# Attention, MoE and FFN on one core: x^T from quarter-array products with a PSUM bank per batch, late arrivals at fixed places, and the third pair's steps later

## The chip, the cores and the metric

The kernel runs on one core of a Trainium2 chip, in one launch. The metric is the device time of that launch in microseconds (us), the median of several executions; lower is better. Engines are named as in the profile: PE is TensorE's matmul side and PEld its weight loads, DVE is VectorE, ACT is ScalarE, POOL is GpSimd, and SP is SyncE, which here issues nearly all DMAs in one queue.

## The reference, cut to what matters

Three layers follow each other: linear attention over 4 batches of 8 heads, 576 tokens and 64 dimensions; a dense mixture of 8 experts with Sinkhorn routing; and a feed-forward network. Tokens are 2304 = 4 x 576, the model width is 512 = 8 x 64.

```
q_s = exp(q - max(q, -1)); q_s /= sum(q_s, -1) + 1e-9        # over the 64 dims
k_s = exp(k - max(k, 2));  k_s /= sum(k_s, 2) + 1e-9         # over the 576 tokens
kv  = einsum('bhsd,bhse->bhde', k_s, v)                      # 64 x 64 for each batch and head
x   = einsum('bhsd,bhde->bhse', q_s, kv) -> (2304, 512)
P   = exp(x @ w_gate - max); 8 times: P /= rows, P /= columns, P *= N / E
out = sum over e of P[:, e] * (relu(x @ w1[e]) @ w2[e])      # w1[e] 512 x 1024, w2[e] 1024 x 512
h   = out @ w_in                                             # 512 x 2048
y   = (h * clip(h + 3, 0, 6) / 6) @ w_out                    # 2048 x 512
```

## The kernel before, in words

The batches are taken two at a time: `attention(0)` (`t0`) holds batches 0 and 1, `attention(1)` (`t1`) batches 2 and 3. The two batches of a pair lie in the two halves of the 128 partitions when kv and x are made. The 18 token tiles form 6 groups of 3 tiles (384 columns), and the groups form three pairs, `PAIRS = [(0, 1), (3, 4), (2, 5)]`. Groups 0 to 2 belong to `t0`, groups 3 to 5 to `t1`, so that the third pair (p = 2) needs both. A column chunk `c` (0 to 3) is 128 of x's 512 columns, that is two heads.

x^T of one `(c, g)` is made by `xset`: q of a group is normalised on POOL (`qn`), transposed on PE (`qtr`, three 128x128 transposes into one PSUM bank), copied by ACT, and multiplied by the scaled kv. Before, that kv lies in `bds`, a block-diagonal array with zeros off its diagonal blocks: four f32 matmuls of 128 rows by 64 columns with 192 moving columns fill one PSUM bank.

Every product of the MoE uses a seven-product (Strassen-like) scheme on halves, with operands split into a high and a low f16 part. `forms(p, ...)` makes the seven x operands of a pair from the x^T banks (`plain` makes a fresh bank, `onto` adds another operand to it by an identity matmul on PE, `out_` writes the high part by ACT and the low part by DVE). The third pair's are combined by `combine_steps` from copies. `w1_steps` and `w2_steps` do the same for a slice of weights: a load into `raw` or `acc`, a maximum over it (`am_a`, `am_b`), a maximum across partitions by a PE broadcast (`across_max`: the column goes to PE as `cm_...`, and DVE reduces the bank), a power of two as the scale (`pow2`), and splits, high by ACT and low by DVE (L217).

The work is a list of steps `(s, p)`: slice `s` of 16 MoE slices and then 4 FFN slices, pair `p`. A step is two up bursts of seven products each (`up_burst`, banks X, Y, Z, or A to D in the FFN), and the down tiles (`y`) of the step ahead of it. All other work hangs on the products: after each one `tick()` takes `rate` entries of the list `ticks`, and one of `side` or `back`. `rate` is 3 in (0, 0), 2 in (1, 0) and then 1. A `None` in a list is a tick in which nothing is issued. In the first six steps of the order the Tile scheduler places instructions; from there on (`tc.manual_schedule()`) they stand as written.

Ahead of (0, 0) stands a prologue: k's maxima and transposes, `ksub`, `kexp`, q's softmax (`qmax`, `qsub`, `qexp`, `qsum`), kv on PE, the first weights' scale, `kvout`, `kvmax` and `kvkeep`, and then `forms` of the first pair. `t1`'s own chain (k, q, kv) runs beside (0, 0) and (1, 0), then `second_pair` makes the second pair's x operands; it ends when (0, 1) starts. PSUM: `ps_u` holds the banks A to D, `ps_d` two banks for `y`, and `ps_m` two banks for everything else (`kT`, `kv`, `qT`, x, forms of the second pair, `cm_...`, Sinkhorn's `csp`).

Of the kernel before, what the change touches and what calls it, by code (L numbers as in the profile page):

```python
# [43 lines left out]
def tile_attention_moe_ffn(  # L44
# [81 lines left out]
    bds = cpool.tile([P, 2, NKC, P], F32, name="bds")  # L126
# [135 lines left out]

    def w1_steps(s, first=False):
# [16 lines left out]
        if first:  # L280
            scale = w_scale(f"a{s}_", st, s, TOP1)
            scale[-1] = (lambda f=scale[-1]: (f(), res[s].__setitem__("s1", st["s"])))
            return load, scale, [
                tt(S1, A[1, 0], A[1, 1], "tensor_add"), tt(S2, S1, A[0, 0], "tensor_sub"),
                tt(A[1, 0], A[0, 0], A[1, 0], "tensor_sub"),
            ], [
                sp(QA11, A[0, 0]), sp(QS2, S2), sp(QS1, S1), sp(QA12, A[0, 1]),
                lambda: (tt(A[0, 1], A[0, 1], S2, "tensor_sub")(), sp(QA22, A[1, 1])()),
                sp(QS3, A[1, 0]), sp(QS4, A[0, 1]),
            ]  # L290
        steps = [load, None, None, None] + w_scale(f"a{s}_", st, s, TOP1)
# [10 lines left out]
    def w2_steps(s, flat=raw):  # L302
# [10 lines left out]
        steps = [load, None, None, None] + w_scale(f"b{s}_", st, s, TOP2, flat)  # L313
# [91 lines left out]
    qbuf = view(half(acc[:, NJ // 2 :, :]), 0, [P, H, QR, D])  # L405

    kt = view(xbuf, X_W, [P, H, QR, D])
# [3 lines left out]
    def attention(pr):  # L411
# [3 lines left out]
        first = pr == 0  # L415
        def rows(src, i):
# [12 lines left out]

        def load_q():  # L430
            load(qbuf, q, slice(0, NKC))
# [21 lines left out]
        def kmax(c):  # L453

            kh = kt[:, 2 * c : 2 * c + 2]
            l1 = view(scr, (c % 2) * DM, [P, 2, 4, D])
# [4 lines left out]
                wide[4][:, c * P : (c + 1) * P].rearrange("p (h d) -> p h d", d=D), l1[:, :, 0], kh[:, :, 8]  # L461
# [14 lines left out]
        def kback(cs):  # L476
# [5 lines left out]
            for n, c in enumerate(cs):  # L482
# [5 lines left out]
                t["kb", c] = ps[:, n * P : (n + 1) * P]  # L488

        def ksub(c):  # L490
            hs = slice(2 * c, 2 * c + 2)
            nc.vector.tensor_tensor(
                out=kt[:, hs], in0=kt[:, hs],
                in1=t["kb", c].rearrange("p (h d) -> p h d", d=D).unsqueeze(2).to_broadcast([P, 2, QR, D]),
# [24 lines left out]
        def kvout():  # L519
# [5 lines left out]
            for j in range(2):  # L525
                for i in range(2):
                    a = slice(i * D, (i + 1) * D)
                    nc.vector.tensor_tensor(
                        out=bds[a, i, :, j * D : (j + 1) * D], in0=t["kv"][j][a, :, :D],
                        in1=rz[a, j].unsqueeze(2).to_broadcast([D, NKC, D]), op=ALU.mult,  # L530
                    )

        def kvmax():
            t["am"] = col("kvm")
            nc.vector.tensor_reduce(
                out=t["am"], in_=bds.rearrange("p i c m -> p (i c m)"), axis=AX, op=ALU.max, apply_absolute_value=True
            )

        def kvkeep():
            nc.vector.tensor_copy(mx[:, pr : pr + 1], st["mm"])  # L540
            pow2(st["mm"], sx[:, pr, :], TOP1)
            nc.scalar.activation(bds[:, 0], bds[:, 0], AF.Copy, scale=sx[:, pr, 0:1])
            nc.vector.tensor_scalar_mul(bds[:, 1], bds[:, 1], sx[:, pr, 0:1])
# [8 lines left out]
        grows = lambda g: slice(gl(g) * GJ, (gl(g) + 1) * GJ)  # L552

        def qmax(g):
            if "qm" not in t:
                t["qm"] = sm.tile([P, H, QR], F32, tag="qm", name=f"qm{pr}", bufs=2)
            nc.vector.tensor_reduce(
                out=t["qm"][:, :, grows(g)], in_=qbuf[:, :, grows(g), :], axis=AX, op=ALU.max
            )

        def qsub(g, eng=nc.vector):
            qh = qbuf[:, :, grows(g), :]
# [3 lines left out]
        def qexp(g):  # L566
            qh = qbuf[:, :, grows(g), :].rearrange("p h r d -> p h (r d)")
            nc.scalar.activation(qh, qh, AF.Exp)

        def qsum(g):  # L570
            if "qs" not in t:
                t["qs"] = sm.tile([P, H, QR], F32, tag="qm", name=f"qs{pr}", bufs=2)
                t["qr"] = sm.tile([P, H, QR], F32, tag="qr", name=f"qr{pr}", bufs=1)
            sv, rv = t["qs"][:, :, grows(g)], t["qr"][:, :, grows(g)]
            nc.vector.tensor_reduce(out=sv, in_=qbuf[:, :, grows(g), :], axis=AX, op=ALU.add)
            nc.vector.tensor_scalar_add(sv, sv, 1e-9)
            nc.vector.reciprocal(rv, sv)
# [743 lines left out]
```

## Time and profile before

| | before |
|---|---|
| device time, median of 3 executions | 1901.04 us (1900.40 to 1901.06) |
| profiled execution, device time | 1901.46 us |
| its span in the profile | 1899.7 us |
| busy: PE / DVE / ACT / POOL | 1845.8 / 1178.0 / 865.8 / 611.1 us |
| mean granted clock of TensorE | 0.991 |

The device time is 1.8 us longer than the span. Busy times are sums over the whole span: they don't tell what ends a wait in one stage. The tables by stretch show the share of each engine in a stretch, the timelines show single instructions with what ended the idle time ahead of them, and the tables of waits sum such idle time by the instruction that waited and by the one that released it. A granted clock (PEclk) of 1.00 is the upper of TensorE's two levels, 2.4 GHz, and 0.50 the lower, 1.2 GHz.

### The profile page before, as it was taken

Reading aid. Unit: us, or ns where it says so; the run is one execution under the profiler, and the core shown is the slowest. Engines: PE = TensorE matmul, PEld = TensorE weight load, DVE = VectorE, ACT = ScalarE, POOL = GpSimd, SP = SyncE. Lnnn points to the kernel's source line nnn. Section 1 sums busy time; section 2 is a strip of 40 time slices with the busy share of each in tenths; the row PEclk is TensorE's granted clock in tenths of the full one; section 3 lists DMA queues with packets and bytes.
Section 4 is the critical chain, followed back from the end, with each engine's and each line's share of the span. In section 5 each row is a group of like instructions: output and inputs, shape, how many; then the busy total and the mean of one; then the engine's idle time right before and its main releaser. Section 6 shows DMA issues by size and latency. Waiting matters only on the chain.

```text
span 1899.7 us, 26823 instructions
## 1 busy us (share of the span) xinstructions
PE 1845.8 (97%) x10596; PEld 976.5 (51%) x10596; DVE 1178.0 (62%) x2109; ACT 865.8 (46%) x1653; POOL 611.1 (32%) x582
## 2 busy tenths in 40 slices
PE   4999999999999999999999999999999999999999
PEld 2555554555555555555555555555555555555554
DVE  8875736565655556565656565565635796768554
ACT  3754434444444444443434444444434466535432
POOL 4342234233342333333333423242332333313121
PEclk8999999999999999999999999999999999999999
DMA  9200001111111202112011111121100100000001
GB/s 294 95 24 1 1 23 56 40 40 56 40 56 40 78 25 71 43 35 73 23 56 39 56 40 58 37 78 33 46 28 1 45 23 23 23 23 23 1 28 72
DMA packets 48430, 87.72 MB, mean 46 GB/s; under 512 B 12208, under 2 KB 12208, under 8 KB 48304
## 3 DMA queue, kind: packets, MB, share of 16 engines
q1 hardware_dynamic: 48304, 86.01, 13.6%
q8 instruction: 83, 1.36, 0.3%
q14 instruction: 43, 0.35, 0.1%
HBM read 72.89 MB, written 13.11 MB: 45 GB/s over the span
## 4 chain that ended last, share of the span: by engine, by line
PE 84%; DVE 11%; ACT 2%; issue 1%; DMA 1%; POOL 0%; SPq 0%; DVEq 0%; ACTq 0%; POOLq 0%
PE y L1028 44%; PE X L928 18%; PE Y L928 9%; PE Z L928 5%; DVE w1buf L217 2%; PE B L928 2%; PE C L928 2%; PE A L928 2%; DVE r L936 1%; PE D L928 1%; DVE acc L1038 1%; DVE g L953 1%; DVE scr L391 1%; DVE xbuf L387 1%; DVE w2buf L217 1%
## 5 line engine op out<-in xcount | busy, mean ns | idle before, releaser
L1028 PE MATMUL y<-w2buf,h 128*128 128x512 f16 x4320 | 992.1, 379 | 0.1
L928 PEld LDWEIGHTS <-w1buf 128*128 128x128 f16 x5040 | 491.1, 98 | 366.4 <-issue 16.4
L1028 PEld LDWEIGHTS <-h 128*128 128x128 f16 x4320 | 422.1, 98 | 470.7 <-issue 4.5
L960 POOL TENSOR_TENSOR h<-r,h 128x384 f16<-128x384 f32 x288 | 273.9, 952 | 869.6 <-ACT h L959 787.5
L928 PE MATMUL X<-xbuf,w1buf 128*128 128x384 f16 x2304 | 440.3, 327 | 1.6 <-ACT r L941 1.1
L941 ACT ACTIVATE r<-X 128x384 f32<-128x384 f32 x384 | 187.0, 487 | 509.7 <-PE X L928 500.2
L1038 DVE SCALAR_TENSOR_TENSOR acc<-y,cf,acc 128x512 f32<-128x512 f32 x252 | 188.0, 746 | 214.3 <-PE y L1028 214.3
L928 PE MATMUL Y<-xbuf,w1buf 128*128 128x384 f16 x1152 | 220.1, 327 | 1.6 <-DVE r L936 0.8
L936 DVE SCALAR_TENSOR_TENSOR r<-Y,r 128x384 f32<-128x384 f32 x192 | 106.0, 552 | 75.5 <-PE Y L928 40.0
L958 ACT ACTIVATE r<-r 128x384 f32<-128x384 f32 x192 | 99.9, 520 | 113.3 <-DVE r L936 112.5
L959 ACT CAST h<-r 128x384 f16<-128x384 f32 x288 | 146.9, 510 | 7.9
L955 POOL TENSOR_TENSOR h<-g,h 128x384 f16<-128x384 f32 x72 | 67.5, 937 | 255.6 <-ACT h L954 200.4
L928 PE MATMUL Z<-xbuf,w1buf 128*128 128x384 f16 x576 | 110.9, 327 | 0.0
L936 DVE SCALAR_TENSOR_TENSOR r<-Z,r 128x384 f32<-128x384 f32 x96 | 53.0, 552 | 91.4 <-PE Z L928 89.4
L962 ACT ACTIVATE h<-r 128x384 f16<-128x384 f32 x96 | 50.2, 522 | 93.1 <-DVE r L936 93.0
L954 ACT CAST h<-g 128x384 f16<-128x384 f32 x96 | 48.9, 511 | 90.6 <-DVE g L953 90.5
L963 DVE SCALAR_TENSOR_TENSOR h<-r,h 128x384 f16<-128x384 f32 x96 | 56.6, 590 | 51.8 <-ACT h L962 51.8
L952 ACT ACTIVATE g<-r,three,zi 128x384 f32<-128x384 f32 x96 | 67.5, 704 | 6.7 <-DVE r L936 5.8
L953 DVE SCALAR_TENSOR_TENSOR g<-g,r 128x384 f32<-128x384 f32 x96 | 60.4, 631 | 13.8 <-ACT g L952 11.1
L936 DVE SCALAR_TENSOR_TENSOR r<-B,r 128x384 f32<-128x384 f32 x48 | 26.6, 554 | 63.6 <-PE B L928 62.0
L928 PE MATMUL C<-xbuf,w1buf 128*128 128x384 f16 x288 | 54.8, 327 | 3.6 <-DVE r L936 3.6
L928 PE MATMUL B<-xbuf,w1buf 128*128 128x384 f16 x288 | 54.6, 326 | 1.7 <-DVE r L936 1.6
(631 smaller groups left out, 1610.7 us busy)
## 6 DMA issues: line engine op xcount, KB each, us to landing
raw<-in_moe_w_dram SPq DMA_DIRECT2D x31, 1024.0 KB, 5.9
scr<-in_moe_w_in_dram SPq DMA_DIRECT2D x16, 512.0 KB, 4.3
scr<-in_moe_w_out_dram SPq DMA_DIRECT2D x16, 512.0 KB, 3.7
acc<-in_q_dram SPq DMA_DIRECT2D x4, 1152.0 KB, 8.4
out_dram<-acc SPq DMA_DIRECT2D x18, 256.0 KB, 2.0
win<-scr SPq DMA_DIRECT2D x16, 256.0 KB, 3.3
wout<-scr SPq DMA_DIRECT2D x16, 256.0 KB, 2.1
raw<-win SPq DMA_DIRECT2D x4, 1024.0 KB, 5.0
```

Source lines behind the costliest of these rows:

```text
L217: nc.vector.scalar_tensor_tensor(out=lo, in0=src, scalar=scale, in1=hi, op0=ALU.mult, op1=ALU.subtract)
L928: nc.tensor.matmul(bank[b], w[:, i, wi, c, fs], x[:, i, xi, c, :], start=(first and n == 0), stop=(last and n == 5), skip_group_check=True,)
L936: nc.vector.scalar_tensor_tensor(out=o, in0=bank[b], scalar=sign * H_DOWN, in1=i1, op0=ALU.mult, op1=ALU.add)
L941: nc.scalar.activation(o, bank[b], fn, scale=H_DOWN)
L952: nc.scalar.activation(r, c, AF.Relu, scale=zi, bias=three)
L953: nc.vector.scalar_tensor_tensor(out=r, in0=r, scalar=6.0 * KAPPA, in1=c, op0=ALU.min, op1=ALU.mult)
L955: eng.tensor_sub(h[:, 1, :], r, h[:, 0, :])
L958: nc.scalar.activation(c, c, AF.Relu)
L959: nc.scalar.copy(h[:, 0, :], c)
L960: eng.tensor_sub(h[:, 1, :], c, h[:, 0, :])
L1028: nc.tensor.matmul(ps, hs[grp][fc][:, hi, ts_], w[:, wi, fc, :], start=(n == 0), stop=(n == 11))
L1038: nc.vector.scalar_tensor_tensor(out=acc[:, j, :], in0=ps, scalar=cf, in1=acc[:, j, :], op0=ALU.mult, op1=ALU.add)
```

## The change

Three edits go together.

1. `bds` is gone. `kvs` holds the scaled kv of both batches without zeros (half the elements, and `kvout`, `kvmax`, `kvkeep` work on half). `xset` now takes two chunks and two banks: each matmul uses 64 rows by 64 columns, the row half is the batch, and each batch has its own bank. `forms` works on a pair of banks with 128x6x64 views of the operands. The number of PE matmuls is the same.
2. The third pair's part of `t0` (group 2: its softmax, its normalising, its products) moves out of the prologue and of (0, 0) into `third_pair`, where `t1`'s group 5 is made. The four `scaled` passes of ACT are dropped, since x is scaled as it leaves PSUM. The last third of q's rows is loaded by itself into `qlast`. `late()` has ACT write one column of head 0's place in it before the DMAs of that head.
3. Loads and maxima get other places. `t1`'s k and v loads stand behind the load of the second slice's w1. Slice 0's w2 has its room in another part of `acc`, and its steps stand after the forms in the prologue. `kmax` takes several chunks at a time. `fill` gives five empty ticks instead of three behind the loads of slices 2 and 3. The step order is (0,0), (1,0), (0,1), (1,1), (0,2), (1,2).

```diff
@@ w1_steps, w2_steps
+    def fill(s):
+        return [None] * (5 if s in (2, 3) else 3)
-        steps = [load, None, None, None] + w_scale(f"a{s}_", st, s, TOP1)
+        steps = [load] + fill(s) + w_scale(f"a{s}_", st, s, TOP1)
@@ attention(pr)
             for j in range(2):
-                for i in range(2):
-                    a = slice(i * D, (i + 1) * D)
-                    nc.vector.tensor_tensor(
-                        out=bds[a, i, :, j * D : (j + 1) * D], in0=t["kv"][j][a, :, :D],
-                        in1=rz[a, j].unsqueeze(2).to_broadcast([D, NKC, D]), op=ALU.mult,
-                    )
+                nc.vector.tensor_tensor(
+                    out=kvs[:, :, j * D : (j + 1) * D], in0=t["kv"][j][:, :, :D],
+                    in1=rz[:, j].unsqueeze(2).to_broadcast([P, NKC, D]), op=ALU.mult,
+                )
...
-        def xset(ps, c, g):
-            p3 = ps.rearrange("p (r n) -> p r n", n=P)
-            q3 = t["qT", c, g].rearrange("p (r n) -> p r n", n=P)
+        def xset(b, cs, g):
+            for n, c in enumerate(cs):
+                q3 = t["qT", c, g].rearrange("p (r n) -> p r n", n=P)
+                for i in range(2):
+                    ai = slice(i * D, (i + 1) * D)
+                    o = b[i].rearrange("p (c r n) -> p c r n", c=2, n=QP)
+                    for j in range(2):
+                        aj = slice(j * QP, (j + 1) * QP)
+                        nc.tensor.matmul(
+                            o[aj, n], kvs[ai, c, aj], q3[ai, :, aj], start=(n == 0), stop=(n == 1),
+                            skip_group_check=True,
+                        )
...
             return [
-                plain(cp, ga, QB11), f_t1, plain(cp + 2, gb, QB22), f_on(QT2, [(minus, QT1)]),
-                plain(cp + 2, ga, QB21), f_on(QT4, [(minus, QB21)]), f_on(QT3, [(plus, QB21), (minus, QB11)]),
+                plain(low, ga, QB11), plain(low, gb, QT1, [(minus, QB11)]), plain(high, ga, QB21),
+                plain(high, gb, QB22), f_on(QT2, [(minus, QT1)]), f_on(QT3, [(minus, QB11)]),
+                f_on(QT4, [(plus, QB11), (minus, QB21)]),
             ]
@@ beside(t1)
+        every = tuple(range(NKC))
+        steps += [
+            lambda: (t["kmax"](every), t["ktr"](every)), K("qmax", ga), lambda: (t["mT"](every, t["kT"]), t["kback"](every)),
+            K("qsub", ga), lambda: (t["ksub"]((0, 1)), t["kexp"](0), t["kexp"](1)), K("qexp", ga),
+            lambda: (t["ksub"]((2, 3)), t["kexp"](2), t["kexp"](3)), K("qmax", gb), K("qsub", gb), K("qexp", gb),
+        ]
@@ third_pair
-    def third_pair(t):
+    def third_pair(t0, t1):
...
-        steps = group_steps(t, gb)
+        steps = [rooms(t0)] + group_steps(t0, ga)
+        steps += t0["items"]([((cp, cp + 2), ga, two(2 * cp), rescale[:, 0:1]) for cp in range(2)])
+        steps += [rooms(t1)] + group_steps(t1, gb)
@@ prologue and order of steps
-        run([f0[0], f1[0], a1[0], f0[1], f1[1], f0[2], f1[2], a1[1], f0[3], f1[3], a1[2], f0[4], f1[4], a1[3],
-             f0[5], f1[5], a1[4], f0[6], f1[6], a1[5], a1[6]])
+        run([f[0], a1[0], f[1], a1[1], f[2], a1[2], f[3], a1[3], f[4], a1[4]] + a2[:6] + [f[5], a1[5]] + a2[6:8]
+            + [f[6], a1[6]] + a2[8:])
+        w1_1 = w1_steps(1)
+        w1_1[0]()
+        t1["load_k"](2)
+        t1["load_v"]()
-    order = [(0, 0), (1, 0), (0, 1), (0, 2), (1, 1), (1, 2)]
+    order = [(0, 0), (1, 0), (0, 1), (1, 1), (0, 2), (1, 2)]
-    it = t0["items"]([(c, third, stage2[:, c], 1.0) for c in range(NKC)])
-    put(ticks, group_steps(t0, third))
+    def late():
+        for t, at in ((t0, qlast[0]), (t1, qlast[1])):
+            nc.scalar.copy(at[:, 0, 0, 0:1], mx[:, 1:2])
+            t["load_qlast"]()
+    put(ticks, [late])
```

How the instructions stand on DVE in the prologue, before, from q's first row sums to the first piece of kmax of `t1` (`qs` and `qr` are q's sums and reciprocals, `am_a` and `am_b` the maxima of slice 0's w1 and w2, `kvm` that of kv):

```order
L575 TENSOR_REDUCE qs_345<-acc 128x8x3
L557 TENSOR_REDUCE qm_188<-acc 128x8x3
L576 TENSOR_SCALAR qs_345<-qs_345 128x8x3
L564 TENSOR_TENSOR acc<-acc,qm_188 128x8x192
L577 RECIPROCAL qr_346<-qs_345 128x8x3
L575 TENSOR_REDUCE qs_345<-acc 128x8x3 x2
...
L246 TENSOR_REDUCE am_a__417<-raw 128x1 x2
L246 TENSOR_REDUCE am_b__598<-acc 128x1
...
L528 TENSOR_TENSOR bds<-kv_199,krz 64x4x64 x2
L528 TENSOR_TENSOR bds<-kv_200,krz 64x4x64 x2
L457 TENSOR_TENSOR scr<-xbuf 128x512
L535 TENSOR_REDUCE kvm<-bds 128x1
```

The same place in the changed kernel (`xbuf` in the L553 rows is `kvs`, which lies there for `t0`):

```order
L598 TENSOR_REDUCE qm_189<-acc 128x8x3
L599 TENSOR_SCALAR qm_189<-qm_189 128x8x3
L600 RECIPROCAL qm_189<-qm_189 128x8x3
L598 TENSOR_REDUCE qm_189<-acc 128x8x3
L599 TENSOR_SCALAR qm_189<-qm_189 128x8x3
L600 RECIPROCAL qm_189<-qm_189 128x8x3
L246 TENSOR_REDUCE am_a__416<-raw 128x1 x2
L254 TENSOR_REDUCE wm_a__419<-am_a__416 128x1
...
L553 TENSOR_TENSOR xbuf<-kv_200,krz 128x4x64
L553 TENSOR_TENSOR xbuf<-kv_201,krz 128x4x64
L560 TENSOR_REDUCE kvm<-xbuf 128x1
```

The third group's maximum, subtraction and sum, both `am_b` rows and the kmax rows of `t1` no longer stand ahead of `kvm`.

The DMAs in SP's queue before, from k's first load to the third slice's w1 (the second `k` and `v` rows are those of `t1`, `raw` holds w1, then w2):

```order
L422 DMA xbuf<-in_k_dram 128x576 x8
L422 DMA acc<-in_q_dram 128x4x576 x2
L422 DMA acc<-in_v_dram 128x576 x8
L272 DMA raw<-in_moe_w_dram 128x4x512
L1105 DMA wg<-in_moe_w_gate_dram 128x4x8
L308 DMA acc<-in_moe_w_dram 128x4x512
L422 DMA xbuf<-in_k_dram 128x2x576 x4
L443 DMA xbuf<-in_v_dram 128x9x64 x8
L272 DMA raw<-in_moe_w_dram 128x4x512
L422 DMA acc<-in_q_dram 128x4x576 x2
```

And in the changed kernel, from q's load on:

```order
L443 DMA acc<-in_q_dram 128x384 x8
L432 DMA acc<-in_v_dram 128x576 x8
L276 DMA raw<-in_moe_w_dram 128x4x512
...
L443 DMA acc<-in_q_dram 128x192 x14
L312 DMA acc<-in_moe_w_dram 128x4x512
L443 DMA acc<-in_q_dram 128x384 x2
L276 DMA raw<-in_moe_w_dram 128x4x512
L432 DMA xbuf<-in_k_dram 128x2x576 x4
L463 DMA xbuf<-in_v_dram 128x9x64 x8
L443 DMA acc<-in_q_dram 128x384 x6
L312 DMA raw<-in_moe_w_dram 128x4x512
L443 DMA acc<-in_q_dram 128x192 x2
```

`t1`'s k and v moved behind the second w1, and of the 16 `qlast` DMAs 14 stand early and 2, those of the marked head, behind the second w2.

On DVE, the last Sinkhorn iteration and the splits of slice 2's w1 (L217), before (`cs` is the column sum that PE's `csp` waits for):

```order
L217 SCALAR_TENSOR_TENSOR w1buf_85<-raw,ws_a__2423,w1buf_85 128x512
L827 TENSOR_SCALAR rs<-rs 128x18
L217 SCALAR_TENSOR_TENSOR w1buf_85<-wtmp,ws_a__2423,w1buf_85 128x512
L829 RECIPROCAL rr<-rs 128x18
L217 SCALAR_TENSOR_TENSOR w1buf_85<-raw,ws_a__2423,w1buf_85 128x512
L830 TENSOR_TENSOR prob<-prob,rr 128x144
L832 TENSOR_REDUCE cs<-prob 128x8
```

And in the changed kernel:

```order
L858 RECIPROCAL rr<-rs 128x18
L202 TENSOR_SCALAR mc<-m_a__2655 128x1
L859 TENSOR_TENSOR prob<-prob,rr 128x144
L204 TENSOR_SCALAR eb<-mc 128x1
L861 TENSOR_REDUCE cs<-prob 128x8
L208 TENSOR_SCALAR ws_a__2672<-eb 128x1
L211 TENSOR_SCALAR ws_a__2672<-eb 128x1
L217 SCALAR_TENSOR_TENSOR w1buf_85<-raw,ws_a__2672,w1buf_85 128x512
```

The last `cs` now stands ahead of the first split instead of behind several.

## Rows read from the trace of the kernel before

**Rows 1.** The page: busy time by engine, and the chain that ended last.

```profile
PE 1845.8 (97%) x10596; PEld 976.5 (51%) x10596; DVE 1178.0 (62%) x2109; ACT 865.8 (46%) x1653; POOL 611.1 (32%) x582
PE 84%; DVE 11%; ACT 2%; issue 1%; DMA 1%; POOL 0%; SPq 0%; DVEq 0%; ACTq 0%; POOLq 0%
```

**Rows 2.** Busy time by stretch, with counts, clock, DMA share and GB/s.

```profile
0.00:62.00 62.00, 31.98 (x422) 21.20 (x423) 54.13 (x101) 26.83 (x42) 21.01 (x27) 0.81 0.75 225
62.00:320.00 258.00, 248.24 (x1792) 134.86 (x1790) 164.23 (x330) 134.41 (x260) 90.45 (x93) 0.99 0.09 31
320.00:1899.70 1579.70, 1565.61 (x8386) 820.41 (x8384) 959.60 (x1680) 704.51 (x1353) 499.59 (x464) 1.00 0.12 42
```

**Rows 3.** The same columns for the prologue's chain.

```profile
18.54:48.22 29.68, 15.31 (x319) 11.95 (x319) 29.58 (x52) 10.24 (x15) 17.88 (x18) 0.69 1.00 267
```

**Rows 4.** Timeline of DVE in the prologue: start, length, instruction, count.

```profile
28.04 1.74 DVE L557 TENSOR_REDUCE qm<-acc 128x24 f32<-128x1536 f32 x1
29.81 1.76 DVE L564 TENSOR_TENSOR acc<-acc,qm 128x1536 f32<-128x1536 f32 x1
31.70 3.35 DVE L575 TENSOR_REDUCE qs<-acc 128x24 f32<-128x1536 f32 x2
...
38.95 1.21 DVE L246 TENSOR_REDUCE am_b__598<-acc 128x1 f32<-128x1024 f32 x1
...
40.37 1.73 DVE L528 TENSOR_TENSOR bds<-kv,krz 64x256 f32<-64x256 f32 x4
...
43.11 1.21 DVE L535 TENSOR_REDUCE kvm<-bds 128x1 f32<-128x1024 f32 x1
```

**Rows 5.** kmax of `t1` (tile scr) on DVE, in one stretch: busy time and count.

```profile
42.10:46.96 4.86, 3.10 (x6) 0.63 0.82 132
```

**Rows 6.** SP's DMA issues in the prologue: start, time to issue, DMAs.

```profile
0.73 3.87 SPq L422 DMA_DIRECT2D xbuf<-in_k_dram  x8
...
23.37 7.41 SPq L422 DMA_DIRECT2D xbuf<-in_k_dram  x4
...
66.17 0.37 SPq L272 DMA_DIRECT2D raw<-in_moe_w_dram  x1
```

**Rows 7.** DMA of the first 35 us: size, median us from issue to landing.

```profile
xbuf<-in_k_dram SPq DMA_DIRECT2D x8, 288.0 KB, 5.5
```

**Rows 8.** Timeline of PE: products of x, of `t1`'s kv, and a second-pair form.

```profile
48.22 2.83 PE L609 MATMUL f<-qt,bds 128*64 128x192 f32 x16 [0.62 <-ACT bds L542]
...
57.75 1.52 PE L609 MATMUL f<-qt,bds 128*64 128x192 f32 x16
...
108.97 1.28 PE L514 MATMUL kv<-xbuf 64*64 64x65 f32 x72
...
126.05 0.87 PE L609 MATMUL f<-xbuf,bds 128*64 128x192 f32 x8
```

**Rows 9.** Line 609 alone (the products of x) after the prologue, columns as PE, PEld.

```profile
62.00:320.00 258.00, 15.54 (x128) 8.29 (x128) 0.99 0.09 31
```

**Rows 10.** PE's waits from 62 to 320 us: in total, times, longest.

```profile
PE csp L837 <- DVE cs L832: 2.7, 1, 2.7
PE cm_kv L193 <- DVE kvm L535: 2.7, 1, 2.7
PE cm_a__3082 L193 <- DVE wm_a__3067 L254: 1.3, 1, 1.3
```

**Rows 11.** PE's waits after 320 us.

```profile
PE cm_b__3319 L193 <- DVE wm_b__3304 L254: 1.8, 1, 1.8
```

**Rows 12.** Busy time from the second w1's load to kvm, then to (0, 1).

```profile
66.20:118.70 52.50, 50.75 (x547) 29.28 (x545) 48.71 (x76) 36.36 (x63) 23.27 (x20) 1.00 0.31 106
118.70:156.00 37.30, 35.77 (x203) 17.98 (x204) 18.80 (x43) 17.95 (x38) 10.37 (x13) 0.95 0.00 1
```

**Rows 13.** Timeline of DVE: the low part of that form.

```profile
127.99 0.56 DVE L633 TENSOR_TENSOR xbuf<-f,xbuf 128x384 f16<-128x384 f32 x1 [0.98 <-ACT xbuf L632]
```

More of the change, by code (lines that the diff above doesn't have):

```diff
@@ L428, in load_k, with load_rows, load_qlast @@
                 load(kt, k, slice(u * NKC // n, (u + 1) * NKC // n))
+        def load_rows(dst, r0, n):
+            for i in range(2):
+                for c in range(NKC):
+                    nc.sync.dma_start(
+                        out=dst[:, 2 * c + i], in_=rows(q, i)[:, c].rearrange("n (r d) -> n r d", d=D)[:, r0 : r0 + n]
+                    )
         def load_q():
-            load(qbuf, q, slice(0, NKC))
+            load_rows(qbuf, 0, GA)
+        def load_qlast():
+            load_rows(qlast[pr], GA, GJ)
         def v_ones():
@@ L552, in attention @@
         grows = lambda g: slice(gl(g) * GJ, (gl(g) + 1) * GJ)
+        qof = lambda g: qbuf[:, :, grows(g), :] if gl(g) < 2 else qlast[pr]
         def qmax(g):
@@ L621, in forms, with batch, both, xmm @@
+        def batch(ap, i):
+            return ap.rearrange("p c (r n) -> p c r n", n=P)[:, :, :, i * QP : (i + 1) * QP]
+        def both(ap):
+            return ap.rearrange("p (c r n) -> p c r n", c=2, n=QP)
+        def xmm(cs, g, dst, scale):
+            b = [psm([P, GN], f"x{cs[0]}_{g}_{i}") for i in range(2)]
+            xset(b, cs, g)
+            for i in range(2):
+                nc.scalar.activation(batch(dst, i), both(b[i]), AF.Copy, scale=scale)
+        def forms(p, bank):
             ga, gb = PAIRS[p]
@@ L635, in onto, with out_ @@
[L635 to L642 removed]
+            def out_(b, qd):
+                for i in range(2):
+                    hi, lo, src = batch(dst[:, qd, 0], i), batch(dst[:, qd, 1], i), both(b[i])
+                    if qd == QT4:
+                        nc.scalar.activation(hi, src, AF.Copy, scale=-1.0)
+                        nc.vector.scalar_tensor_tensor(
+                            out=lo, in0=src, scalar=-1.0, in1=hi, op0=ALU.mult, op1=ALU.subtract
+                        )
+                    else:
+                        nc.scalar.copy(hi, src)
+                        nc.vector.tensor_tensor(out=lo, in0=src, in1=hi, op=ALU.subtract)
@@ L643, in f, with onto, plain @@
+            def onto(b, qds):
+                for i in range(2):
+                    for m, qd in qds:
+                        for hl in range(2):
+                            nc.tensor.matmul(
+                                both(b[i]), m, batch(dst[:, qd, hl], i), start=False, stop=True, skip_group_check=True
+                            )
+            def plain(cs, g, qd, qds=()):
                 def f():
-                    ps[qd] = bank(f"f{p}_{cp}_{qd}")
-                    xset(ps[qd], c, g)
+                    ps[qd] = [bank(f"f{p}_{qd}_{i}", qd, i) for i in range(2)]
+                    xset(ps[qd], cs, g)
+                    onto(ps[qd], qds)
```

216 lines of the change are left out of this document (80 added, 136 removed).

## The prediction, made before the changed kernel ran

> **What bounds the kernel now.** I read the page first. PE is busy for 1845.8 us of the span of 1899.7, and the chain that ended last lies on PE for 84% and on DVE for 11% [rows 1]. The table by stretch then says where the rest is [rows 2]: up to 62 us PE is busy for 31.98 us only, at a mean granted clock of 0.81, and DVE for 54.13; from 62 to 320 us PE lacks 9.8 us, and from 320 us to the end 14.1. So there are two places where time can be won: the prologue, which is not PE's, and the single waits and single matmuls behind it, where PE is nearly always busy and each us of its work or idle time counts in full.
>
> In the prologue the table of one stretch settles the engine. From q's first maximum (18.54) to the first product of x (48.22) DVE is busy 29.58 of 29.68 us [rows 3]. What leaves DVE there brings the first product forward, unless something else is then late. DMA is the candidate: its share in this stretch is 1.00 as well [rows 3].
>
> **The prologue.** From DVE's path go: the third group's maximum, subtraction and one of two sums, 1.74 + 1.76 + 3.35/2 = 5.18 us; both halves of w2's maximum, 2 x 1.21 = 2.42 [rows 4]; the k maxima of `t1`, 3.10 [rows 5]; half of the `bds` writes, since two of 256 elements stand for four, 1.73/2 = 0.87; and half of kvm, 1.21/2 = 0.61 [rows 4]. That is 12.2 us. Two things come back. Behind kvm, which ended at 44.32, only some 1.0 of the 3.10 us of k maxima had been done; I infer it from the 42.1 to 43.11 ahead of kvm. The other 2.1 us filled gaps of a chain of tiny instructions that goes to PE and back, and that chain stays; they are not saved. And the maximum of k's chunks 2 and 3 is now one: it needs the last of eight k DMAs, issued by 0.73 + 3.87 = 4.60 [rows 6] and landing some 5.5 us later [rows 7], at about 10.1; I take 0.7 us for that. The first product comes 12.2 - 2.1 - 0.7 = 9.4 us earlier, at about 38.8. The bounds: 12.2 if both givebacks are covered, and half of the 9.4 if the DMAs set the pace (a rival, below).
>
> What was removed here is not all removed from the kernel. w2's maximum and its splits now stand beside the forms of the first pair, and the third group goes to steps where PE has product after product; DVE is busy 164.23 of 258 us there [rows 2], so it has room. `late()` puts one ACT copy and two DMAs (the marked head) behind that copy in SP's queue, and the load of slice 2's w1 behind both; that load is needed only two steps later, and I cost it at nothing. If ACT reached the marker late, SP's queue would hold back w1 of slice 2, and its cover (the steps of slices 0 and 1) is over 50 us.
>
> **The products of x.** Behind the prologue 128 matmul records make x [rows 9], 16 sets of 8. Back to back 16 records take 1.52 us, 95 ns each [rows 8], so a set takes 0.76, and all take 12.2 us. After, a pair of chunks takes 16 records on quarters of the array. The trace has quarter-array matmuls already: 72 records of 65 columns in 1.28 us, 17.8 ns each [rows 8]; scaled by columns, 192 take 52.5 ns, and 16 records 0.84 us. Half of today's 95 ns gives 0.76. I take 0.80, so 8 pairs take 6.4 us: -5.8. The `onto` matmuls keep their columns, the transposes their number.
>
> **Waits that go.** Slice 2's w1 splits no longer stand between the last Sinkhorn iteration's row and column sums, so that PE's wait for `cs`, 2.7 us, should go; two empty ticks more behind the loads of slices 2 and 3 should take the waits for their maxima, 1.3 [rows 10] and 1.8 [rows 11]. Sum -5.8. Each of these stalls was PE's alone, in a row that PE reached too early; nothing else I see is late behind them.
>
> **Waits that come.** First `cm_kv` of `t1`. From the second w1's load, 66.17 [rows 6], which follows the first pair's splits and so moves to about 56.8, DVE had 48.71 us of work in 52.5, and PE 50.75 [rows 12]. After, `t1`'s k and v are loaded only behind that w1, where before they had been issued at 23.37 [rows 6]. DVE gets the 3.10 of k maxima and loses 0.87 + 0.61: 50.3 us of work. PE loses four sets of the third group, 4 x 0.76 = 3.0, to a later stretch: 47.7. DVE's own gaps were 52.5 - 48.7 = 3.8; with these kvm starts 54.1 us behind the load. PE's idle time in that stretch was 1.75, of which the wait ahead of kvm was part. The wait of 2.7 [rows 10] grows by DVE's 1.6 and PE's 3.0: +4.6.
>
> Second, the second pair's forms. A bank was held from the first product, 126.05 [rows 8], to the end of DVE's low part, 127.99 + 0.56 = 128.55 [rows 13]: 2.5 us. The pool has two banks; a set now takes both, and the next transpose needs one. Other work (the down tiles) stands between, so that I charge a third of 2.5 for each of the four sets: +3.3. Bounds are 0 (all covered) and 4 x 2.5 = 10.
>
> Third, smaller ones that no row prices: four chunks' transposes in one go, the group of the third pair that waits for the two marked DMAs: +2.0, between 0 and the 3.6 of twice the `cm_b` wait.
>
> **The sum** against the profiled execution's 1901.46 us: -9.4 - 5.8 - 5.8 + 4.6 + 3.3 + 2.0 = -11.1, so 1890.4; the median of the runs shown lies 0.4 under the profiled execution, so 1890 for the median. 0.2%, about what a measurement of this kernel can tell from no change, is 3.8 us.
>
> **Rivals.**
> (a) `t1`'s chain becomes the bound, and the kernel slower. Place: the wait of `cm_kv`. Four k DMAs took 7.41 us to issue [rows 6] and stand behind a 1 MB load; k's maxima, transposes, subtractions, kv and kvm then follow in turn, with DVE filled by the w1 splits. For it: DVE was 93% busy there already (48.71 of 52.5). Against it: PE has the products of two whole steps to do meanwhile. The forecast gains 11.1; it is eaten, and 3.8 more, when this wait reaches 2.7 + 4.6 + 15 = 22 us, that is, when kvm comes over 69 us behind the load instead of 54. Time 1905 and more.
> (b) The quarter products gain nothing, since the banks and not the array set the pace, or since the two row halves do not run at once: 16 records then take 1.52 as today. Time 1890 + 5.8 = 1896. Against it: from 118.7 to 156 us, DVE is busy 18.80 and ACT 17.95 of 37.3 us, PE 35.77 [rows 12], so that the evicting engines have room; and kv's 17.8 ns for 65 columns are well under 95 x 65/192 = 32 ns [rows 8], so that row halves do overlap. The Trainium skill, TensorEngine Tiling (Array Packing), Performance Considerations (PSUM Bottleneck), says that tiling speeds up the array but not the emptying of PSUM, which may become the bottleneck. By that rule the time would be the 1896 of this case; the rows agree with it for the latency of one bank (2.5 us against 0.87 of product) and not for the engines' load.
> (c) The prologue gains only half, because DMA is the next bound there: v, w1, and the smaller q loads with 16 more DMAs in the queue. For it: the share of 1.00 [rows 3]. Against it: much of that traffic is `t1`'s k and v, issued from 23.37 on [rows 6], which leaves the stretch. Time 1890 + 4.7 = 1895.
> (d) The waits that come are covered: 1890 - 9.9 = 1880.
>
> **How the numbers follow.** I give the forecast 0.53 (its own range 1884 to 1895), (a) 0.09, (b) 0.14, (c) 0.13 and (d) 0.11. (b) and (c) together, or either with a little of (a), end within 0.2% (1897.2 to 1904.8): 0.10 in all; 0.08 of (a) ends slower; the rest, 0.82, faster. The range for 8 in 10 runs from 1880, case (d), to 1898, a little above (b) and (c).
>
> **What would show it.** Right: the first product of x near 38.8 us and the second w1's load near 56.8; 16 records of a pair in 0.75 to 0.85 us; no wait for `cs`, nor for the maxima of slices 2 and 3; a wait of some 7 us at `cm_kv`, and short waits of `qT` or x products on DVE's low parts in the second pair. Wrong: a first product later than 43 us (c), 16 records in 1.5 us (b), a wait of 15 us or more at `cm_kv` or at kT (a), or a new wait for slice 2's w1 behind the marked DMAs, for which I charged nothing.

## The result, and the profile after

The changed kernel takes 1877.92 us (median of 4 executions, 1876.73 to 1879.02) against 1900.72 for the kernel before, run beside it. The ratio is 0.9883, with a 95% interval of 0.9865 to 0.9900. The forecast was 1890 with a range of 1880 to 1898: the direction is right, and the gain is about twice what was forecast. The profiled execution took 1879.02 us, 22.4 less than the profiled execution before.

The page of the changed kernel, busy time and chain [rows 1 before]:

```profile
PE 1830.8 (98%) x10596; PEld 969.0 (52%) x10596; DVE 1171.2 (62%) x2086; ACT 864.5 (46%) x1651; POOL 609.8 (32%) x581
PE 86%; DVE 9%; ACT 2%; issue 1%; POOL 1%; DMA 0%; SPq 0%; DVEq 0%; POOLq 0%; ACTq 0%
```

PE's busy time itself fell by 15.0 us, its idle time by 7.5. To see where, I cut both traces at the same four events: the first product of x, the first up product, the start of (0, 1) and the start of (2, 0). The kernel before, stretch by stretch (columns as in [rows 2]):

```profile
0.00:48.22 48.22, 19.70 (x339) 13.87 (x339) 42.14 (x77) 15.71 (x21) 20.06 (x26) 0.81 0.97 290
48.22:60.58 12.36, 10.86 (x75) 6.46 (x76) 10.57 (x22) 9.90 (x19) 0.36 (x1) 0.78 0.00 1
60.58:155.89 95.31, 91.96 (x784) 50.41 (x782) 73.08 (x128) 58.45 (x109) 34.91 (x33) 0.98 0.17 59
155.89:277.63 121.74, 116.63 (x797) 63.80 (x796) 66.12 (x160) 59.18 (x118) 37.15 (x40) 0.99 0.03 10
277.63:1899.70 1622.07, 1606.68 (x8607) 841.95 (x8605) 986.05 (x1724) 722.51 (x1387) 518.57 (x484) 1.00 0.12 41
```

And the changed kernel:

```profile
0.00:38.05 38.05, 16.38 (x334) 11.42 (x335) 29.36 (x53) 13.96 (x19) 15.18 (x22) 0.90 0.77 255
38.05:45.34 7.29, 6.59 (x69) 3.89 (x69) 5.15 (x10) 4.59 (x10) 0.35 (x1) 0.59 0.20 72
45.34:137.97 92.63, 84.64 (x748) 46.90 (x749) 85.23 (x137) 58.06 (x106) 30.55 (x27) 0.98 0.32 90
137.97:257.88 119.91, 116.72 (x842) 64.67 (x840) 70.54 (x165) 63.58 (x129) 47.11 (x49) 1.00 0.05 18
257.88:1877.20 1619.32, 1606.48 (x8607) 842.12 (x8605) 980.90 (x1723) 724.27 (x1388) 516.61 (x484) 1.00 0.12 41
```

The second number of each row is the length. Beside the differences stands what the terms of the forecast make of the same stretches: the second pair's eight sets and the third group's four leave or shrink in the third stretch (12 x 0.76 to 4 x 0.80, -5.9), where the waits that come were to cost 4.6 + 3.3 and half of the 2.0; the other half, the third group's four sets by pairs (+0.2) and the wait for `cs` (-2.7) fall into the fourth, slice 3's waits (-3.1) into the last.

| stretch | measured, us | forecast, us |
|---|---|---|
| up to the first product of x | -10.2 | -9.4 |
| from there to the first up product | -5.1 | 0 |
| (0, 0) and (1, 0), to the start of (0, 1) | -2.7 | +3.0 |
| to the start of (2, 0) | -1.8 | -1.5 |
| the rest | -2.8 | -3.1 |
| sum | -22.5 | -11.0 |

Two rows carry nearly the whole miss, the second and the third. PE's waits of the changed kernel from 62 to 320 us [rows 10 before]:

```profile
PE y L1057 <- POOL h L989: 2.7, 1, 2.7
PE Y L957 <- DVE xbuf L391: 2.0, 2, 1.0
PE qT L615 <- POOL xbuf L606: 1.2, 2, 0.7
PE cm_b__892 L193 <- DVE wm_b__878 L254: 1.1, 1, 1.1
PE kT L491 <- DVE scr L484: 0.8, 1, 0.8
PE X L957 <- ACT r L970: 0.7, 1, 0.7
PE csp L866 <- DVE cs L861: 0.4, 1, 0.4
```

The waits for `cs` (but 0.4) and for slice 3's maxima are gone, as forecast. The wait at `cm_kv`, forecast at over 7 us, is not there at all; other waits have come, the longest a down tile's for POOL.

PE's timeline of the changed kernel at the places named in the prediction [rows 8 before]:

```profile
38.05 2.84 PE L635 MATMUL f<-qt,xbuf 64*64 64x192 f32 x32 [1.65 <-ACT xbuf L567]
...
42.21 2.43 PE L635 MATMUL f<-qt,xbuf 64*64 64x192 f32 x32
...
68.13 1.04 PE L1057 MATMUL y<-w2buf,h 128*128 128x512 f16 x2 [2.69 <-POOL h L989]
...
111.08 0.23 PE L193 MATMUL cm_kv<-identb,kvm 128*128 128x128 bf16 x1
```

SP issued the second w1's load at 56.51 [rows 6 before], where 56.8 was forecast:

```profile
56.51 0.38 SPq L276 DMA_DIRECT2D raw<-in_moe_w_dram  x1
```

Products of x alone, changed kernel, by the same stretches (PE busy and count, then PEld):

```profile
38.05:45.34 7.29, 5.27 (x64) 3.45 (x64) 0.59 0.20 72
45.34:137.97 92.63, 4.66 (x64) 3.02 (x64) 0.98 0.32 90
137.97:257.88 119.91, 4.42 (x64) 2.39 (x64) 1.00 0.05 18
```

And before, where the first row is the first pair, whose 64 records the sum had left out:

```profile
48.22:60.58 12.36, 8.29 (x64) 5.45 (x64) 0.78 0.00 1
60.58:155.89 95.31, 11.52 (x96) 6.17 (x96) 0.98 0.17 59
155.89:277.63 121.74, 4.02 (x32) 2.12 (x32) 0.99 0.03 10
```

They fell by 3.0 us in the first pair, where PE partly ran at the lower clock, and from 15.54 to 9.08, by 6.5, behind it.

### The profile page after: what moved, and what is told of

Read it like the earlier page. It is cut to its first block, busy times and chain, and to the rows that moved or that the text cites. A ratio compares the mean times of both kernels' runs of the same rounds, so it can differ in the third digit from the quotient of the medians.

```text
span 1877.2 us, 26846 instructions
## 1 busy us (share of the span) xinstructions
PE 1830.8 (98%) x10596; PEld 969.0 (52%) x10596; DVE 1171.2 (62%) x2086; ACT 864.5 (46%) x1651; POOL 609.8 (32%) x581
## 4 chain that ended last, share of the span: by engine, by line
PE 86%; DVE 9%; ACT 2%; issue 1%; POOL 1%; DMA 0%; SPq 0%; DVEq 0%; POOLq 0%; ACTq 0%
PE y L1057 45%; PE X L957 19%; PE Y L957 9%; PE Z L957 5%; PE B L957 2%; PE C L957 2%; PE A L957 2%; DVE w1buf L217 1%; DVE r L965 1%; PE D L957 1%; DVE g L982 1%; DVE scr L395 1%; DVE acc L1067 1%; DVE xbuf L391 1%; PE qT L615 0%
```

## The experiments

Each ratio below is against the kernel before; its interval is about plus or minus 0.0015 to 0.0018, some 3 us, so where less is at stake the length of a stretch in the profile decides, and the text says which. The stretch from (0, 1) to (2, 0) repeats to 0.3 us or better between runs with the same order and ticks, what follows it to 0.8 us. The changed kernel is "after"; a difference to it is the difference of two ratios times 1901 us.

**Products doubled, first pair.** After, with one line changed:

```diff
-                    xset(ps[qd], cs, g)
+                    for _ in range(2 if p == 0 else 1):
+                        xset(ps[qd], cs, g)
```

> The changed kernel with each of the first pair's four product sets issued twice, 64 matmul records more; the result is the same. Theory A (PE sets the stretch between the first product of x and the first up product, so that halving these products gave the first step its early start): in the changed kernel 32 records took 2.84 us there at a granted clock of 0.5, so four sets more cost about 5.7 us, the first up product goes from 45.3 to some 50 or 51 us, and the time rises by 4 to 5.7 us, to 1882 to 1884. Theory B (the splits and the reads of the banks by ACT and DVE set this stretch, and the early start comes from the order alone): the first up product moves by less than 1.5 us, and the time by 0 to 1.5.

1880.73 us, ratio 0.9896 (0.9881 to 0.9911), 2.5 above after. The stretch from the first product to the first up product (37.61 to 47.16) grew from 7.29 to 9.55 us, PE busy 9.24 of it:

```profile
37.61 5.40 PE L635 MATMUL f<-qt,xbuf 64*64 64x192 f32 x64 [1.65 <-ACT xbuf L567]
...
44.02 2.83 PE L635 MATMUL f<-qt,xbuf 64*64 64x192 f32 x64
```

Between the theories: PE, busy for nearly all of it, sets the doubled stretch, but the second half of the doubled sets ran at the full clock (64 records in 2.83 us, where 32 had taken 2.43 in after), so that they cost 2.3 us and not 5.

**Products doubled, the other pairs.** The same with `p == 1` and in `xmm`.

> The changed kernel with the eight product sets of the second and third pair issued twice, 128 records more; the result is the same. Theory A (a set counts in full on PE, as the sum of the prediction had it): a set stood for 0.8 to 1.3 us in the changed kernel, so the time rises by 6.5 to 9 us, to 1884 to 1887. Theory B (two banks of the pool set the pace of these stretches): the further products lie in time in which PE would wait anyway, and the time rises by 0 to 2.5 us.

1885.77 us, ratio 0.9925 (0.9910 to 0.9940), 8.0 above after, which is theory A's size. In the profile the two stretches from the first up product (43.66) to (2, 0) grew by 5.8 and 2.5 us. PE's busy time grew by 3.6 and 2.6 of these, 48 ns for each of the 128 records more. The rest is idle time, for the most part two waits of the transposes for DVE's low parts, which after does not have:

```profile
117.45 0.52 PE L615 MATMUL qT<-ident,xbuf 128*128 128x128 f32 x3 [0.34 <-DVE xbuf L671]
...
125.15 0.52 PE L615 MATMUL qT<-ident,xbuf 128*128 128x128 f32 x3 [1.63 <-DVE xbuf L671]
```

So x products lie on PE's path in full. Of the banks this run says less than its theories had it, since a doubled set also holds its two banks for longer: a pool of two banks could lengthen these stretches as well. That the banks do not set the pace in after is read from after itself, further down.

**The same sets in another order.** Within a set, all four matmuls of one batch's rows ahead of the other's:

```diff
-            for n, c in enumerate(cs):
-                q3 = ...
-                for i in range(2):
+            for i in range(2):
+                ...
+                for n, c in enumerate(cs):
+                    q3 = ...
```

> The changed kernel with the same 16 records in each product set, but issued with all matmuls of the first batch's rows ahead of those of the second, so that neighbours in PE's queue use the same half of the rows; the result is the same. Theory A (the gain of the quarter products is that two row halves run at once): a set takes about 1.5 us as two sets did before the change, against 0.8 to 1.3; the eight later sets cost 3.7 to 5.7 us more and the first pair's four 1 to 2, so the time rises by 5 to 7 us, to 1883 to 1885. Theory B (the gain has to do with the smaller stationary operand or with the banks, not with running at once): less than 1.5 us.

1879.03 us, ratio 0.9886 (0.9871 to 0.9901), 0.6 above after: no difference. The first two sets, at the lower clock, start at 37.08 and take as long as in after (2.84):

```profile
37.08 2.89 PE L635 MATMUL f<-qt,xbuf 64*64 64x192 f32 x32 [1.64 <-ACT xbuf L567]
...
39.90 1.46 PE L676 MATMUL f<-xbuf,minus 128*128 128x384 f16 x4
```

Theory A's forecast failed; it had taken for granted that halves overlap only when they alternate. That they overlap is not refuted: 32 records from 37.08 to 39.90 are 88 ns each at the lower clock, against 163 for the 16 records from 48.22 to 50.83 before, at the same level. The order within a set doesn't matter; whether the gain needs two halves at once was not tried in another way, and is not shown.

**DVE work put back into the prologue.** The second half of w1's maximum is taken three times, and then nine times (`a1_scale[1]` repeated):

```diff
-        run(a1_scale[:3])
+        run([a1_scale[0]] + [a1_scale[1]] * 9 + [a1_scale[2]])
```

> The changed kernel with the second half of w1's maximum in the prologue taken three times instead of once: two more DVE instructions of about 1.2 us ahead of kvm; the result is the same. Theory A (DVE alone sets the prologue, as the prediction had it, also after the change): the first product of x goes from 38.05 to about 40.4 us, and the time rises by 2.4 us. Theory B (DMA or the round trips to PE set it now): less than 0.8 us on both.

> The changed kernel with the second half of w1's maximum taken nine times instead of once in the prologue, eight more DVE instructions of about 1.14 us, 9.1 us in all, near what the change took from DVE there; the result is the same. Theory A (DVE sets the prologue, behind a slack of about 1.2 us in which it waits for PE's broadcast in the changed kernel; the run with two more fits that): the first product of x comes 7.9 us later, near 46, and the time rises by 7.5 to 8.5 us. Theory B (only a part of DVE's time counts there, as 1.1 of 2.3 us did with two more): 4 to 5 us.

With two more: 1879.44 us, ratio 0.9889 (0.9872 to 0.9905), 1.1 above after; the first product at 38.95. With eight more: 1886.21 us, ratio 0.9924 (0.9909 to 0.9939), 7.8 above after; the first product comes at 46.00, 7.95 later:

```profile
41.93 0.29 PE L193 MATMUL cm_a__442<-identb,wm_a__427 128*128 128x128 bf16 x1 [7.53 <-DVE wm_a__427 L254]
43.81 0.29 PE L193 MATMUL cm_kv<-identb,kvm 128*128 128x128 bf16 x1 [1.59 <-DVE kvm L560]
46.00 2.84 PE L635 MATMUL f<-qt,xbuf 64*64 64x192 f32 x32 [1.90 <-ACT xbuf L567]
```

So the prologue's length is DVE's, us for us, once a slack of some 1.2 us is used up. After shows that slack on DVE itself, behind kvm:

```profile
33.85 0.69 DVE L560 TENSOR_REDUCE kvm<-xbuf 128x1 f32<-128x512 f32 x1
35.71 0.29 DVE L195 TENSOR_REDUCE m_a__436<-cm_a__434 128x1 f32<-128x128 f32 x1 [1.17 <-PE cm_a__434 L193]
```

**`t1`'s k and v loaded early again**, ahead of the first pair's forms (the two calls moved up).

> The changed kernel with the second batch pair's k and v loaded ahead of the first pair's forms and of the second w1, as before the change, some 20 us earlier. Theory A (the loads' place does not matter, since kvm came just in time and the wait for it has gone because PE has more to do ahead of it): within 1 us of 1877.9. Theory B (the later loads are part of the gain, since early ones hold back w2 or the second w1): slower by 2 to 6 us. Theory C (the prediction's: the later loads made the chain to kvm late): faster by 1 to 3 us, the waits at cm_b and kT of 1.1 and 0.8 us gone.

1877.68 us, ratio 0.9881 (0.9867 to 0.9896). Theory A: PE got to `cm_kv` at 101.65 instead of 111.08, again without a wait, and the way from the first up product to (0, 1) stayed the same, 92.57 us (43.57 to 136.14) against 92.63:

```profile
101.65 0.23 PE L193 MATMUL cm_kv<-identb,kvm 128*128 128x128 bf16 x1
```

So kvm came 9.4 us earlier, and the way to (0, 1) got no shorter: the place of the loads does not set it. PE stands idle for some 8 us on that way in both runs, at other instructions, and DVE is as busy as PE (85.23 and 84.64 of 92.63 us in after, where it was 73.08 and 91.96 of 95.31 before). Which of the two sets the length now was not tried.

**Three empty ticks instead of five**, behind the loads of slices 2 and 3 (after with `fill` as 3).

> The changed kernel with three empty ticks behind the loads of slices 2 and 3 again, instead of five. Theory A (the two further ticks took away the waits at the two broadcasts of slice 3's maxima): these waits come back, 1.3 and 1.8 us as before the change, and the time rises by 3.1 us, to 1881. Theory B (they went because the whole first part is earlier or ordered otherwise): no wait, 0 to 1 us.

1883.85 us, ratio 0.9913 (0.9898 to 0.9928), 5.7 above after, nearly twice theory A. Not only slice 3's waits came back; so did the one for `cs`:

```profile
PE csp L866 <- DVE cs L861: 3.0, 2, 2.6
...
PE cm_a__3077 L193 <- DVE wm_a__3062 L254: 1.5, 1, 1.5
```

The stretch from (0, 1) to (2, 0) grew by 4.6 us (119.91 to 124.54) and what follows by 3.3. The prediction had put the end of the `cs` wait down to the new order of DVE, which is true, but that order hangs on the ticks.

**The order of steps as before**, with slice 2's w1 asked for at (1, 1), as the kernel before has it; the change also asks for it later, at (1, 2).

> The changed kernel with the order of steps as before, (0,1), (0,2), (1,1), (1,2), and slice 2's w1 asked for at (1,1). In its built order DVE's last column sum still stands ahead of slice 2's w1 splits. Theory A (the order of steps took away the wait for that sum): the wait of 2.7 us and the stretch at the lower clock that followed it before come back, the time rises by 3 to 4.4 us. Theory B (it is the later third pair, or DVE's order within the tick lists, and the order of steps is worth nothing by itself): within 1 us of 1877.9.

1880.70 us, ratio 0.9898 (0.9882 to 0.9915), 2.9 above after. Neither theory: the wait for `cs` stayed away, yet the stretch from (0, 1) to (2, 0) took 122.46 us against 119.91, with 1.1 us more of PE's own time and 1.5 more of waits. What in the order costs this was not taken apart.

**The ticks alone, in the kernel before:**

```diff
-        steps = [load, None, None, None] + w_scale(...)
+        steps = [load] + [None] * (5 if s in (2, 3) else 3) + w_scale(...)
```

> The kernel before with one edit of the change alone: five empty ticks behind the loads of slices 2 and 3. In its built order the last column sum now stands ahead of slice 2's w1 splits. Theory A (the two ticks by themselves take away the waits of 2.7, 1.3 and 1.8 us, and with the first of them the stretch at the lower clock that follows it, some 1.7 us): 7 to 7.5 us faster than the kernel before. Theory B (the prediction's sum, with no price on the clock, if all three go): 5.8 us faster. Theory C (the wait for the column sum needs the new order of steps too): 3.1 us faster.

1893.48 us against 1900.82, ratio 0.9961 (0.9946 to 0.9976): 7.4 us from two empty ticks at four loads. Theory A. By stretches, 121.74 became 117.27 (-4.5) and 1622.07 became 1619.56 (-2.5):

```profile
155.27:272.54 117.27, 114.86 (x797) 63.31 (x796) 66.52 (x160) 59.07 (x118) 37.37 (x40) 1.00 0.03 10
272.54:1892.10 1619.56, 1606.49 (x8607) 842.10 (x8605) 981.64 (x1724) 724.02 (x1387) 516.68 (x484) 1.00 0.13 41
```

The first of these lost the wait of 2.7 us and 1.8 us of PE's busy time (116.63 to 114.86), for the same 797 matmuls: that is the lower clock behind the wait. The same stretch took 119.91 us in the changed kernel, so that the other edits together cost 2.6 us there.

**The ticks split by slice.** Three ticks for slice 2 alone, and for slice 3 alone.

> The changed kernel with three empty ticks behind the loads of slice 2 and five behind those of slice 3. Theory A (a wait of 2.6 us for the column sum comes back and 1.7 us of lower clock behind it): 4 to 4.6 us slower than the changed kernel, in the profile from the start of (0,1) to that of (2,0) alone. Theory B (the wait alone): 2.6 us.

> The changed kernel with three empty ticks behind the loads of slice 3 and five behind those of slice 2. Theory A (two waits of 1.5 and 1.7 us come back, too short to be followed by a stretch at the lower clock): 3.0 to 3.2 us slower than the changed kernel, all of it behind the start of (2,0), no stretch at the lower clock there. Theory B (each wait is followed by lower clock as the long ones are): 5 us or more.

Slice 2: 1883.62 us, ratio 0.9910 (0.9895 to 0.9925). The stretch from (0, 1) to (2, 0) took 122.86 us, 2.95 more than after, with the same wait of 2.64 as with both slices at three; a further 2 us came behind (2, 0), with a wait of 1.5 at slice 3's w2. Slice 3: 1881.88 us, ratio 0.9901 (0.9884 to 0.9917); the stretch up to (2, 0) stayed at 119.91, and the rest grew by 3.5. Of the two waits at slice 3's maxima only the one at w2's came back, with 2.0 us, and the clock stayed at 1.00 behind it. So slice 3 is near theory A in time, though not by two waits. Slice 2 is not: the wait came back without the lower clock, in the one execution that was profiled, the fastest of four. The stretches just behind that wait, with both slices at three:

```profile
244.30:247.70 3.40, 1.30 (x9) 0.91 (x10) 2.88 (x6) 1.56 (x3) 1.44 (x2) 1.00 0.00 0
247.70:251.10 3.40, 3.40 (x12) 1.54 (x11) 3.15 (x11) 0.64 (x2) 1.16 (x2) 0.50 0.00 0
```

and with slice 2 alone:

```profile
243.40:246.80 3.40, 1.33 (x9) 0.93 (x10) 2.88 (x6) 1.52 (x3) 1.40 (x2) 1.00 0.00 0
246.80:250.20 3.40, 3.40 (x20) 1.76 (x18) 3.37 (x12) 1.30 (x3) 1.51 (x3) 1.00 0.00 0
```

Behind nearly the same 1.3 us of work in 3.4, PE got 12 matmuls done at 0.50 and 20 at 1.00 (PEclk is the third column from the end). The whole stretch differs by 124.54 - 122.86 = 1.7 us.

**The first w1's splits later** among the forms, as before the change:

```diff
-        run([f[0], a1[0], f[1], a1[1], f[2], a1[2], f[3], a1[3], f[4], a1[4]] + a2[:6] + [f[5], a1[5]] + a2[6:8]
-            + [f[6], a1[6]] + a2[8:])
+        run([f[0], f[1], a1[0], f[2], f[3], a1[1], f[4], a1[2], a1[3]] + a2[:6] + [f[5], a1[4]] + a2[6:8]
+            + [f[6], a1[5], a1[6]] + a2[8:])
```

> The changed kernel with the splits of the first w1 later among the first pair's forms, about as before the change: the first behind two form stages, the second behind four, the rest behind five and more. Theory A (the stretch from the first product of x to the first up product shrank from 12.4 to 7.3 us partly because a split now follows each form): it grows by 1.5 to 2.5 us, and the time by 1 to 2.5 us. Theory B (it shrank for the products' halving and the number of instructions alone): less than 0.7 us on both.

1881.68 us, ratio 0.9900 (0.9886 to 0.9915), 3.2 above after. The time is a little over theory A's, the place is not theory A's: the first up product came no later (6.40 us behind the first product, in a run with less of the lower clock there), and (0, 0) and (1, 0) took 2.6 us more (95.26 against 92.63). The splits' place matters, but not for the stretch that I had tried to explain by it.

**Versions that might be faster.** In after, slice 0's w2 steps stand between the last of the first pair's forms. Three runs: the steps behind all forms; the same, and behind the second w1's load too; and the first of these with k and v early.

```diff
+        run([f[0], a1[0], f[1], a1[1], f[2], a1[2], f[3], a1[3], f[4], a1[4], f[5], a1[5], f[6], a1[6]] + a2)
```

> The changed kernel with slice 0's w2 steps (maximum, scale, splits) behind all forms and w1 splits of the first pair, not between them. Theory A (in the first step PE waits because the second w1 is late: its load waits for the last split out of the same room, behind w2's maximum on DVE): that load goes from 56.5 to 54 us or sooner, the wait of 1.0 us behind w2's broadcast goes, and the time falls by 1 to 3 us. Theory B (the first step is bound by PE): within 1 us.

> As the run with w2's steps last, but written behind the load of the second w1 too, so that the scheduler ranks that load ahead of them. Theory A (the second w1's load sets the first steps): as that run or 0.5 us better. Theory B (the first step's down tiles need w2, and now come late): slower by 1 us or more than that run.

> w2's steps last and the second batch pair's k and v loaded early, both together. Theory A (k's and v's loads lie in nobody's way): the time of the run with w2's steps last alone, within 1 us. Theory B (with the first steps shorter, the chain to kvm is late): faster than that run by 1 to 3 us.

1877.22 (ratio 0.9877, 0.9862 to 0.9892), 1878.90 (0.9885, 0.9870 to 0.9900) and 1877.45 us (0.9877, 0.9860 to 0.9893): none can be told from after. In the first, SP issued the second w1's load at 50.86 instead of 56.51, and the waits changed their names (from 36 to 150 us):

```profile
PE qT L615 <- POOL xbuf L606: 2.5, 2, 2.2
PE y L1057 <- POOL h L989: 1.8, 1, 1.8
PE y L1057 <- DVE w2buf L217: 1.7, 2, 1.5
```

The way from the first up product to (0, 1) took 93.71 us against 92.63, so a part of what the earlier start gave was lost there.

## Why the prediction was wrong, point by point

**The prologue was right**, in place, mechanism and nearly in size: -10.2 for -9.4, the second w1's load at 56.51 for 56.8, and DVE's work put back moves the first product one for one, behind the slack of 1.2 us. Rival (c), DMA, fell: its share up to the first product is 0.77 now, against 0.97, and the time is DVE's.

**"The first product comes 9.4 us earlier" was the wrong thing to carry forward.** The sum let everything behind it move by the same amount, and so took the stretch up to the first up product as fixed at 12.4 us. It is 7.3. The change shortens the first pair's 64 records as well, from 8.29 to 5.27 us; I had counted only the 128 behind the prologue. The rest of the 5.1 us is 1.3 us of PE for seven `onto` matmuls that now stand behind it (75 records became 69, of which 68 are of these two kinds) and idle time, 1.5 us before and 0.7 after. Doubling the products brought 2.3 us of it back, so that their length counts in this stretch.

**The term of the other sets was near by luck:** 6.5 us less for 5.8. Both of its sizes were too small. The 128 records took 15.54 us before [rows 9], where the sum had 12.2 by the time of sets that stand back to back, and 9.08 after, 1.1 us for 16 records, where it had 0.80. The two errors nearly cancel in the difference.

**`cm_kv`, forecast at +4.6, is the other step that failed.** The forecast had a wait of some 7 us there, and it is not there. kvm did begin 53.8 us behind the load of the second w1, at 110.34 (54.1 forecast), and DVE was busy 50.53 us (50.3 forecast) from that load to `cm_kv`. But the sum took what stands on either engine ahead of `cm_kv` from the order before, although the built order was at hand. Before, kvm began 8.5 us behind the last product of kv, which ended at 110.25 [rows 8], since DVE took a maximum and a subtraction of q and the maxima of slice 2's w1 in between; PE ran out of matmuls:

```profile
118.75 1.21 DVE L535 TENSOR_REDUCE kvm<-bds 128x1 f32<-128x1024 f32 x1
120.02 0.23 PE L193 MATMUL cm_kv<-identb,kvm 128*128 128x128 bf16 x1 [2.70 <-DVE kvm L535]
```

After, it began 1.7 us behind that product, and 13 matmuls cover the way to `cm_kv`:

```profile
102.47 6.16 PE L541 MATMUL kv<-xbuf 64*64 64x65 f32 x288
108.56 1.15 PE L957 MATMUL Y<-xbuf,w1buf 128*128 128x384 f16 x6
109.55 1.67 PE L1057 MATMUL y<-w2buf,h 128*128 128x512 f16 x7
...
110.34 0.68 DVE L560 TENSOR_REDUCE kvm<-kvs 128x1 f32<-128x512 f32 x1
```

In the run with k and v early kvm began 43.9 us behind the load (100.91 and 56.99), so no fixed sum of DVE's work sets its place, and that the 54.1 came out is partly luck. From the load to `cm_kv` PE was busy 49.67 us (47.7 forecast) and idle 4.9, but at other instructions: 2.7 at a down tile, 1.1 at w2's broadcast, 0.8 at `kT`. That stretch took 54.57 us after and 53.85 before. What the sum missed stands behind it: from `cm_kv` to (0, 1) 35.87 us became 26.89, 9.0 less, where its terms (3.3 and 1.0, less 2.9 for the second pair's sets) make some 1.4 more. Ahead of `cm_kv` PE had done 60 records of the down tiles and 159 of the up products before, and 79 and 168 after. These 28 matmuls, 7.7 us by the busy time of their two lines (19.64 + 32.33 against 14.27 + 30.02), no longer stand behind it. This is read from the two traces; no run puts the order back by itself. Rival (a) had no ground: with kvm 9.4 us earlier the time stayed the same.

**The second pair's forms, +3.3, were mis-sized.** From `cm_kv` to (0, 1) PE was idle for 1.2 us in all, at transposes that wait for POOL; the down tiles stand between the sets and cover the banks:

```profile
111.08:137.97 26.89, 25.71 (x175) 13.81 (x175) 23.95 (x44) 13.98 (x28) 8.83 (x9) 1.00 0.03 9
```

Rival (b), that the banks set the pace and the products gain nothing, fell by this row and by the products' own times. The Trainium skill, TensorEngine Tiling (Array Packing), Performance Considerations (PSUM Bottleneck), says that emptying PSUM may become the bottleneck once the array is faster. Here it did not, though it is not far: DVE is busy 23.95 of these 26.89 us, and with the sets doubled PE waited 2.0 us for DVE's low parts.

**The waits that go, -5.8, were right in mechanism and too small in size.** The ticks alone gave 7.4 us in the kernel before (7.0 by the two stretches). The difference is the price that I did not put on a wait: behind the 2.7 us at `cs` PE ran 3.4 us at a granted clock of 0.50, and the same matmuls took 1.8 us longer. Behind the vanished `cm_kv` wait the clock also was 0.50 in the kernel before (122.0 to 125.3); what that cost was not measured. In its profile the changed kernel too has such a stretch, behind the 2.7 us at the down tile (0.50 from 68.0 to 71.4).

**What stays open:** why the new order of steps is worth some 2.5 us between (0, 1) and (2, 0), whether PE or DVE sets the way to (0, 1) now, and what moving the third group is worth by itself. Its DVE share in the prologue is priced by the work put back (one for one behind the slack); its cost in `third_pair` was not taken apart.

## What to carry to other kernels

Cut both traces at the same events, and forecast each stretch, not only the events: the stretch that I left "as it is" held nearly a quarter of the gain, since an edit that shortens an operation shortens it in every place, the prologue too. A wait between two chains needs both chains in the new order; to take either engine's work from the old one is to assume that the scheduler did nothing. And look for collisions in time between two lists of work on one engine before anything larger: two empty ticks at four loads were worth 7.4 us alone in the old kernel, and taking them out of the new one cost 5.7 of its 22.8.

## What the runs showed of the hardware that was not expected

A wait of PE can cost more than its length. Behind the wait of 2.6 to 2.7 us for `cs` the granted clock was 0.50 (1.2 GHz) for 3.4 us in the kernel before and in the run with three ticks for both slices, which cost 1.8 and 1.7 us; behind waits of 1.5 to 2.0 us at slice 3 it stayed at 1.00. But it is not sure: the same wait of 2.64 us with the same work around it was followed by the full clock in the run with slice 2 alone at three ticks. The wait of 2.7 to 2.9 us at the down tile stands in the profiles of after and of ten other runs; in nine of these eleven the clock fell to 0.50 behind it, and in two (the order of steps as before, eight more in the prologue) it stayed at 1.00. So a gain that includes such a stretch holds for the executions that have it.

Four f32 matmuls (eight records) of one half of the rows can stand ahead of those of the other half without a loss: the first two sets took 2.89 us in that order and 2.84 in the alternating one.
